# Seven products instead of eight blocks in the second product of a fused attention and MLP kernel, with w_in streamed from DRAM

## The chip, the cores and the metric

The kernel runs on one core of one Trainium2 chip. The metric is device microseconds of one execution. The engines are TensorE (PE; its weight loads are shown as PEld), VectorE (DVE), ScalarE (ACT), GpSimd (POOL, hardly used here) and SyncE (SP, whose queue issues nearly all DMAs).

## The reference

Eight batches, each of 8 heads, 512 tokens and 32 state rows, head width 64. Tokens attend to the state rows and the state rows to the tokens; the results of both stand side by side and go through two products with a mish between them.

```python
# x: [8, 8, 512, 64], state: [8, 8, 32, 64], w_in: [512, 2048], w_out: [2048, 512]
a = softmax(x @ state.T / 8);   xread = a @ state        # tokens read the state
a2 = softmax(state @ x.T / 8);  sread = a2 @ x           # state rows read the tokens
t = concatenate([xread, sread], axis=2)                  # to [8 * 544, 512]
h = t @ w_in
out = (h * tanh(softplus(h))) @ w_out                    # mish, then the second product
```

## The kernel before, in words

The first product is folded: `sw_slice` (PE tiles `swp`) multiplies the state rows of a batch with slices of `w_in`, and `gemm1` (PE tiles `ph`) multiplies the attention weights `ah`/`al` with that. Every operand of a large product is split into a high part in float32r and a low part, and three matmuls (high by high, high by low, low by high) stand for one. The names end in h and l: `swh`/`swl`, `gh`/`gl`, `ah`/`al`.

A batch is worked in eight slots j; a slot holds two of the 16 chunks of 128 columns of d_ff. In a slot PE runs `gemm1` for the slot (12 matmuls of 512 columns), ACT applies mish from the two `ph` banks, DVE casts the high part (`gh<-g`) and subtracts the low part (`gl<-g,gh`) on 128x1024, and PE runs the second product `gemm2` (PE tiles `acc`) of an earlier slot: 4 token tiles x 2 chunks x 3 = 24 matmuls of 512 columns, whose weights (the stationary side) are blocks of `gh`/`gl` and whose moving side is `wo`. The lag is two slots (`LAG`): a slot's `gh`/`gl` have some 8 us between their making and their use. The four `acc` banks hold the four token tiles of a batch over all eight slots.

PE's order is the program's order: the class `InOrder` chains each PE instruction behind the last. For batch 0 the order of DVE and ACT is written out by hand too (the long string of steps); from batch 1 on a scheduler with a timeline of its own orders DVE, ACT and the DMA queue by program order among what it takes to be ready, and `behind(...)` holds single pieces back. At run time each engine works its own list strictly in order.

Beside the products each batch prepares the next one: transposes of x on DVE (`x_turned`, moved by eight DMAs into `x_rows`), scores (PE tile `sc`, in slot 3), two softmaxes (`soft2` after slot 3, `soft1` after slot 4; `soft1` ends with `soft1_a`, which makes `ah`/`al`, double-buffered), 16 small DMAs that turn `e2T` (after slot 5), the state rows' read (`srp`, in slot 3 of the next batch), and the `sw_slice`s: two in slot 3 and two in slot 7. Between batches 6 and 7 the state rows' own product runs as key "s" (`gemm1_s`, PE tiles `ph_s` and `acc_s`). `w_in` stays in SBUF in whole (`w_in_sb`). The tag "raw" has two buffers of 8 KB a partition, for `x_turned`, `x_rows` and the x of the batch after next. The tag "t" has five buffers of 128x512, for the softmaxes' temporaries.

## Time and profile before

| | |
|---|---|
| median of 3 runs | 643.96 us (643.93 to 644.2) |
| span of the profiled execution, first to last instruction | 642.2 us |
| time of the profiled execution beside its span | not recorded apart; the median is 1.7 us above the span |
| PE, PEld, DVE, ACT busy | 635.1, 509.2, 350.8, 256.6 us |
| granted TensorE clock | 1.000 |
| one batch in the steady part (228.1 to 299.7 us) | 71.60 us |
| matmuls of the second product: `acc`, `acc_s` | 1536 and 96, all of 512 columns |

A busy time is the union of an engine's instructions. Matmuls are pipelined, so the time that one takes from the stream is the distance between two starts, not its duration. In a row of the timeline "x4" means four instructions merged, of which the start of the first is given; the start of the next row then ends them.

### The profile page before, as it was taken

The page shows a single profiled execution, that of the slowest core. Times are in us where ns is not written, and L with a number is a line of the kernel's source. Part 1 is how long each engine was busy: PE and PEld are TensorE (multiplying, and loading weights), DVE is VectorE, ACT ScalarE, POOL GpSimd, SP SyncE. Part 2 cuts the span into 40 slices and gives each one's busy share as a digit, 9 for nine tenths or more (in the row PEclk, how much of TensorE's full clock was granted, in tenths as well). Part 3 has the DMA queues.
Part 4 walks back from the last instruction along what each step waited for, and adds up shares of the span by engine and source line. Part 5 has one row for each costly group of instructions (what it writes and reads, how often), then busy time and mean ns, then how long its engine had stood idle before and what let it go on. Part 6 is the DMA issues. An engine that isn't in the chain of part 4 may idle for free.

```text
span 642.2 us, 10938 instructions
## 1 busy us (share of the span) xinstructions
PE 635.1 (99%) x4523; PEld 509.2 (79%) x4523; DVE 350.8 (55%) x564; ACT 256.6 (40%) x419; POOL 0.7 (0%) x6
## 2 busy tenths in 40 slices
PE   8999999999999999999999999999999999999997
PEld 5777787787878888787878788787878788878886
DVE  5999983665339253665349252755359366432222
ACT  4999852542226122532226212622236336221110
POOL 0000000000000000000000000000000000000000
PEclk9999999999999999999999999999999999999999
DMA  8996717210431033211431033211221001000001
GB/s 326 411 322 183 241 41 205 76 33 15 122 106 53 12 74 132 67 33 31 139 94 36 7 75 131 69 31 40 93 76 47 8 0 67 0 17 17 1 0 65
DMA packets 52129, 56.15 MB, mean 87 GB/s; under 512 B 13297, under 2 KB 41713, under 8 KB 52081
## 3 DMA queue, kind: packets, MB, share of 16 engines
q1 hardware_dynamic: 51648, 55.27, 27.4%
q8 instruction: 35, 0.57, 0.4%
q10 hardware_dynamic: 432, 0.20, 0.1%
q14 instruction: 14, 0.11, 0.1%
HBM read 34.54 MB, written 8.91 MB: 68 GB/s over the span
## 4 chain that ended last, share of the span: by engine, by line
PE 98%; DMA 1%; DVE 0%; SPq 0%; ACT 0%; issue 0%
PE acc L70 55%; PE ph L70 27%; PE swp L70 5%; PE ph_s L70 3%; PE acc_s L70 3%; PE sc L70 1%; PE srp L70 1%; DMA x<-in_x_dram 1%; PE scT L70 0%; SPq L131 0%; DVE scs L70 0%; DVE xT L70 0%; DVE al L70 0%; DVE mx L70 0%; ACT o L70 0%; ACT ah L70 0%
## 5 line engine op out<-in xcount | busy, mean ns | idle before, releaser
L70 PE MATMUL acc<-wo,gh 128*128 128x512 f32 x1024 | 317.9, 392 | 0.0
L70 PEld LDWEIGHTS acc<-wo,gh 128*128 128x128 f32 x1024 | 190.7, 188 | 46.1 <-issue 7.0
L70 PE MATMUL acc<-wo,gl 128*128 128x512 f32 x512 | 199.4, 389 | 0.0
L70 ACT ACTIVATE g<-ph 128x512 f32<-128x512 f32 x128 | 73.6, 597 | 216.7 <-DVE gl L70 199.8
L70 DVE CAST gh<-g 128x1024 fp32r<-128x1024 f32 (+1 forms) x61 | 41.3, 678 | 137.8 <-PE acc L70 131.2
L70 PEld LDWEIGHTS acc<-wo,gl 128*128 128x128 f32 x512 | 96.1, 188 | 20.4
L70 DVE TENSOR_TENSOR gl<-g,gh 128x1024 fp32r<-128x1024 f32 (+1 forms) x65 | 78.4, 1207 | 4.6
L70 PE MATMUL ph<-ah,swh 128*128 128x512 f32 (+1 forms) x260 | 79.8, 389 | 0.0
L70 PE MATMUL ph<-al,swh 128*128 128x512 f32 (+1 forms) x260 | 79.4, 387 | 0.2 <-DVE al L70 0.2
L70 PE MATMUL ph<-ah,swl 128*128 128x512 f32 (+1 forms) x260 | 79.5, 387 | 0.0
L70 DVE TENSOR_TENSOR swl<-swp,swh 128x512 fp32r<-128x512 f32 (+1 forms) x72 | 40.9, 624 | 37.3 <-ACT swh L70 37.2
L70 PEld LDWEIGHTS ph<-ah,swh 128*128 128x128 f32 x260 | 48.2, 188 | 11.8 <-issue 1.2
L70 ACT ACT_TABLE_LOAD x35 | 44.9, 1283 | 30.6 <-DVE s L70 15.7
L70 PEld LDWEIGHTS ph<-al,swh 128*128 128x128 f32 x260 | 48.5, 188 | 10.5 <-DVE al L70 0.4
L70 PEld LDWEIGHTS ph<-ah,swl 128*128 128x128 f32 x260 | 48.6, 188 | 10.2
L70 ACT CAST swh<-swp 128x512 fp32r<-128x512 f32 (+1 forms) x72 | 33.9, 549 | 31.8 <-PE swp L70 31.8
L70 PE MATMUL swp<-w_in_sb,bd 64*32 64x256 f32 x1024 | 33.1, 380 | 0.0
L70 DVE COPY o<-acc 128x512 f32<-128x512 f32 x16 | 11.0, 688 | 32.8 <-PE acc L70 20.0
L70 ACT COPY o<-acc 128x512 f32<-128x512 f32 (+1 forms) x17 | 9.5, 563 | 47.7 <-PE acc L70 30.4
L70 PEld LDWEIGHTS swp<-w_in_sb,bd 64*32 64x32 f32 x1024 | 18.1, 106 | 9.5 <-issue 4.3
L70 DVE TENSOR_SCALAR scs<-sc 128x512 f32<-128x512 f32 (+1 forms) x9 | 5.6, 631 | 29.9 <-PE sc L70 29.9
L70 PE MATMUL acc_s<-wo,gh_s 128*128 128x512 f32 x64 | 19.9, 392 | 0.0
(90 smaller groups left out, 430.6 us busy)
## 6 DMA issues: line engine op xcount, KB each, us to landing
x<-in_x_dram SPq DMA_DIRECT2D x32, 256.0 KB, 3.8
...
out_dram<-o SPq DMA_DIRECT2D x31, 256.0 KB, 2.5
x_rows<-x_turned SPq DMA_DIRECT2D x56, 128.0 KB, 2.4
x_in<-in_x_dram SPq DMA_DIRECT2D x24, 256.0 KB, 3.7
e2T<-u SPq DMA_DIRECT2D x128, 32.0 KB, 1.9
x_again<-in_x_dram SPq DMA_DIRECT2D x8, 256.0 KB, 5.5
```

Source lines behind the costliest of these rows:

```text
L70: made = method(*args, **kwargs)
```

## The change

In batches 2 to 7 and in key "s" the second product is made by pairs of token tiles. A unit is one slot of one pair: 2 chunks of d_ff by 2 token tiles, so 2 by 2 blocks of g, against 2 chunks by 2 halves of `wo`. For the slots 0 to 4 (`SEVEN = 5`) the unit is multiplied by the seven products of Strassen's method in Winograd's form: each product has 3 matmuls (the split) of 256 columns, where the unit had 12 of 512. For the slots 5 to 7 a unit keeps its 12 matmuls of 512 columns. `prepare` makes a unit's operands: three sums on DVE, two casts on ACT and two low parts on DVE with seven products; one cast and one low part, both on DVE, without. `gh` and `gl` now hold one unit each and have two buffers.

The four `acc` banks now belong to one pair ("one", "two", "top", "end"), and a sweep goes through all eight slots for one pair, then for the other. So the units of the second pair wait: g is kept as float32 in up to ten buffers (`UNITS`), and mish is four instructions of 256 columns instead of two of 512. At each point where half a slot's second product stood, one unit is now consumed, if one is ready: in batch 2 one a slot from slot 3 on, then two a slot, and ten remain after the last slot of batch 7. After the seven-product slots, four small instructions gather the banks "one" and "two" into `sums`; at the end of a sweep each tile's result is one DVE addition or subtraction instead of a copy.

The sums of the blocks of `wo` (`seven_weights`, for slots 0 to 4) are made in batch 1 from slot 3 on, one slot at a time; they take the place of `w_in_sb`. `w_in` is first written to DRAM (4 DMAs of 1 MB) and then read back in slices of 1 MB, four for each of the batches 2 to 7 and four for "s", mostly through the tag "raw". The `sw_slice`s of slot 3 are spread over slots 3 and 5 in batches 2 to 6. `ah` and `al` lose their second buffer: `soft1_a`, now `soft1_parts`, moves to the end of slot 7, after the last `gemm1` that reads them. `swh`/`swl` have two pairs of buffers. x of the batch after next is loaded after slot 7 instead of slot 5, and `sreads_moved` of batch 6 moves from slot 5 to slot 6.

```diff
+UNITS = 10
+SEVEN = 5
+G = 4 * P
...
-    w_in_sb = const.tile([P, NC, DF], F32, name="w_in_sb")
+    w_in_sb = const.tile([P, NC, DF], F32, tag="w_in", name="w_in_sb")
+    w_in_again = dram.tile([P, NC, DF], F32, name="w_in_again")
...
-                small["a"] = [pool.tile([P, 2, S], F32R, tag=t, name=f"{t}_{b}") for t in ("ah", "al")]
+                small["a"] = [pool.tile([P, 2, S], F32R, tag=t, name=f"{t}_{b}", bufs=1) for t in ("ah", "al")]
...
-            whole(soft1_n(), *(soft1_a(kc) for kc in two))
+            whole(soft1_n())
+        def soft1_parts():
+            whole(*(soft1_a(kc) for kc in two))
...
+    def load_w_in_again(g, tag="raw", bufs=2):
+        w = pool.tile([P, NC, G], F32, tag=tag, name=f"w_in_{g}", bufs=bufs)
+        last["again"] = nc.sync.dma_start(w, w_in_again[:, :, g * G:(g + 1) * G])
+        return w
...
-        hi = pool.tile([P, 2, n * 2 * P], F32R, tag="swh", name=f"swh_{b}_{j}", bufs=3)
-        lo = pool.tile([P, 2, n * 2 * P], F32R, tag="swl", name=f"swl_{b}_{j}", bufs=3)
+        if n == 2 or j % 2 == 0:
+            sw_pairs[b] = [pool.tile([P, 2, 4 * P], F32R, tag=t, name=f"{t}_{b}_{j}") for t in ("swh", "swl")]
+        at = j % 2 * 2 * P
+        hi, lo = (t[:, :, at:at + n * 2 * P] for t in sw_pairs[b])
...
+    def result(key, t, acc, sums=None, op=None):
+        if (key, t) == (B - 1, NT - 1):
+            last_o = pool.tile([P, DM], F32, tag="e2T", name=f"o_{key}_{t}", bufs=1)
+            for i, part in enumerate((slice(0, 256), slice(256, 512))):
+                o = last_o[:, part]
+                dve.tensor_tensor(o, acc[:, part], sums[:, i], op)
+                (nc.scalar if part.start else nc.sync).dma_start(
+                    out[key * T:key * T + S, part].rearrange("(p t) e -> p t e", t=NT)[:, t, :], o)
+            return
+        o = pool.tile([P, DM], F32, tag="o", name=f"o_{key}_{t}", bufs=2)
+        if sums is not None:
+            dve.tensor_tensor(*(a.rearrange("t (h e) -> t h e", h=2) for a in (o, acc)), sums, op)
+        elif t % 2 == 0:
+            dve.tensor_copy(o, acc)
+        else:
+            act.copy(o, acc)
+        store(key, t, o)
...
+    A12, A22, A11, A21 = range(4)
+    S1, S3, S2, S4 = range(3, 7)
+    T3, T4, T2 = range(3)
+    wx = []
+    def seven_weights(j):
+        if not wx:
+            wx.append(const.tile([P, SEVEN, 2, 3, 256], F32R, tag="w_in", name="wx"))
+        w = pool.tile([P, 4, 256], F32, tag="wt", name=f"w_sums_{j}", bufs=1)
+        dve.tensor_add(
+            w.rearrange("p (k e) c -> p k (e c)", k=2), as_f32(wo[j][:, :, 0]), as_f32(wo[j][:, :, 1]))
+        dve.tensor_sub(w[:, 0], w[:, 0], w[:, 1])
+        dve.tensor_sub(w[:, 1], w[:, 3], w[:, 1])
+        dve.scalar_tensor_tensor(w[:, 3], w[:, 3], -1.0, w[:, 0], ALU.mult, ALU.subtract)
+        dve.tensor_add(w[:, 2], w[:, 2], w[:, 3])
+        low, high = (wo[j][:, 0, n, 256:] for n in range(2))
+        act.copy(high, w[:, 0])
+        dve.tensor_sub(low, w[:, 0], as_f32(high))
+        low, high = (wx[0][:, j, n] for n in range(2))
+        act.copy(high, w[:, 1:])
+        dve.tensor_sub(low, w[:, 1:], as_f32(high))
+    def products(j):
+        left, right = slice(0, 256), slice(256, 512)
+        if j < SEVEN:
+            return [
+                (A11, "one", left, wo[j][:, 0, :, left]), (S2, "one", right, wx[0][:, j, :, T2]),
+                (S3, "two", left, wx[0][:, j, :, T3]), (S1, "two", right, wo[j][:, 0, :, right]),
+                (A12, "top", left, wo[j][:, 1, :, left]), (S4, "top", right, wo[j][:, 1, :, right]),
+                (A22, "end", left, wx[0][:, j, :, T4])]
+        return [
+            (a, bank, slice(0, 512), wo[j][:, k])
+            for bank, blocks in (("top", (A11, A12)), ("end", (A21, A22))) for k, a in enumerate(blocks)]
...
+            if key == 1:
+                beside += [sw_slice(key, 4, 2, first_bank, misc), sw_slice(key, 6, 2, misc, first_bank)]
+            else:
+                beside += [sw_slice(key, 4, 2, first_bank, misc, w=wis[key, 2])]
+        if j == 5 and more and key > 1:
+            beside += [sw_slice(key, 6, w=wis[key, 3])]
+        if j == 2 and not more:
+            beside += [sw_slice(key, 4, bank=first_bank, w=wis[key, 2]), sw_slice(key, 6, w=wis[key, 3])]
+        if j == 7 and more:
+            beside += [sw_slice(key + 1, 0, w=wis[key + 1, 0])]
+            beside += [sw_slice(key + 1, 2, bank=first_bank, w=wis[key + 1, 1])]
...
+        if key == 1 and j < 2:
+            for g in range(2 * j, 2 * j + 2):
+                nc.sync.dma_start(w_in_again[:, :, g * G:(g + 1) * G], w_in_sb[:, :, g * G:(g + 1) * G])
+        if key == 1 and 3 <= j < 3 + SEVEN:
+            seven_weights(j - 3)
...
+        if more and key > 1 and j == 2:
+            wis[key, 2] = load_w_in_again(2)
+        if not more and j == 0:
+            wis[key, 2], wis[key, 3] = load_w_in_again(2), load_w_in_again(3)
...
+            if key > 1:
+                wis[key, 3] = load_w_in_again(3)
...
+            wis[key + 1, 0] = load_w_in_again(0)
...
+            wis[key + 1, 1] = load_w_in_again(1)
...
+        if more and j == 7:
+            own["parts"]()
+            if key + 2 < B:
+                load_x_in(key + 2)
...
+    def mish_units(key, j, phs):
+        for p in range(2):
+            u = new_unit(key, p, j)
+            for k, ph in enumerate(phs):
+                last["mish"] = act.activation(
+                    u[:, 1 - k].rearrange("f h t -> f (h t)"), ph[:, p * 2 * P:(p + 1) * 2 * P], AF.Mish)
+    def prepare():
+        if not todo or todo[0] not in made:
+            return
+        unit = todo.pop(0)
+        key, p, j = unit
+        u = made.pop(unit).rearrange("f k h t -> f (k h) t")
+        hi, lo = (pool.tile([P, 7, P], F32R, tag=t, name=f"{t}_{key}_{p}_{j}") for t in ("gh", "gl"))
+        n = 3 if j < SEVEN else 4
+        if j < SEVEN:
+            sums = temp(f"sums_{key}_{p}_{j}").rearrange("f (s t) -> f s t", s=4)
+            dve.tensor_add(sums[:, :2], u[:, 1:3], u[:, 3:].to_broadcast([P, 2, P]))
+            dve.tensor_add(sums[:, 2], sums[:, 0], u[:, 2])
+            dve.tensor_add(sums[:, 3], sums[:, 2], u[:, 0])
+            act.copy(hi[:, :n], u[:, :n])
+            act.copy(hi[:, n:], sums)
+            low_g(u[:, :n], hi[:, :n], lo[:, :n])
+            low_g(sums, hi[:, n:], lo[:, n:])
+        else:
+            dve.tensor_copy(hi[:, :n], u)
+            low_g(u, hi[:, :n], lo[:, :n])
+        parts[unit] = hi, lo
+        ready.append(unit)
...
+    def consume():
+        if not ready:
+            return
+        unit = ready.pop(0)
+        key, p, j = unit
+        hi, lo = parts.pop(unit)
+        if j == 0:
+            spans[key, p] = {n: second_bank(f"acc_{key}_{p}_{n}") for n in ("one", "two", "top", "end")}
+        banks = spans[key, p]
+        for i, (a, bank, to, w) in enumerate(products(j)):
+            for n, (g, h) in enumerate(((hi, 1), (hi, 0), (lo, 1))):
+                fresh = (key, p, bank) not in begun_banks
+                begun_banks.add((key, p, bank))
+                last["PE"] = pe.matmul(
+                    banks[bank][:, to], g[:, a], w[:, h], start=fresh,
+                    stop=(n == 2 and (j == SLOTS - 1 and i % 2 == 1 or j == SEVEN - 1 and i < 4)), skip_group_check=True)
+            e = banks.get("sums")
+            if j == SLOTS - 1 and i == 1:
+                result(key, 2 * p, banks["top"], e[:, ::2], ALU.add)
+            if j == SLOTS - 1 and i == 3:
+                result(key, 2 * p + 1, banks["end"], e[:, 1::2], ALU.subtract)
+        if j == SEVEN - 1:
+            e = spans[key, p]["sums"] = pool.tile([P, 4, 256], F32, tag="wt", name=f"sums_{key}_{p}", bufs=1)
+            one, two = (banks[n].rearrange("t (h e) -> t h e", h=2) for n in ("one", "two"))
+            act.copy(e[:, 0], one[:, 0])
+            dve.tensor_add(e[:, 3], e[:, 0], one[:, 1])
+            dve.tensor_add(e[:, 1:3], two, e[:, 3:].to_broadcast([P, 2, 256]))
+            dve.tensor_add(e[:, 3], e[:, 1], two[:, 1])
+    def two_next():
+        for _ in range(2):
+            if not todo or (ready and todo[0][2] == 0):
+                return
+            prepare()
+    def halves():
+        if pending:
+            return [lambda: second((0, 1), True), lambda: second((2, 3))]
+        return [consume, consume]
+    for key in [*range(2, B - 1), "s", B - 1]:
+        for j in range(4 if key == "s" else SLOTS):
+            one, other = halves()
+            if key == "s":
+                if j == 0:
+                    one()
+                    sread_transposed()
+                    other()
+                for r in range(2):
+                    gemm1_s(j, r, wis["s", j], new_unit("s", 0, 2 * j + r))
+                    if j:
+                        (one, other)[r]()
+                if j < 2:
+                    wis["s", j + 2] = load_w_in_again(j + 2, *(() if j else ("x", 1)))
+            else:
+                mish_units(key, j, gemm1(key, j, aTs[key], sw))
+                one()
+                around(key, j)
+                other()
+                after(key, j)
+            two_next()
+    while ready or todo:
+        while ready:
+            consume()
+        two_next()
```

More of the change, by code (lines that the diff above doesn't have):

```diff
@@ L514, in soft2 @@
                 whole(soft2_e(kc))
-        own.update(soft1=soft1, soft2=soft2, turn=e2_turned)
+        own.update(soft1=soft1, parts=soft1_parts, soft2=soft2, turn=e2_turned)
         return own
@@ L522, in srT_parts @@
     def srT_parts(bs, values):
-        hi, lo = (t[:, :, bs.start * NS:bs.stop * NS] for t in srT)
+        hi, lo = (t[:, :, bs.start * NS:bs.stop * NS] for t in srT[:2])
         act.copy(hi, values)
@@ L540, in sreads_split @@
     def sreads_split():
+        both = pool.tile([P, NC, 2, B * NS], F32R, tag="raw", name="srT", bufs=2)
+        srT.extend(both[:, :, i] for i in range(2))
+        srT.append(both)
         srT_parts(early, srds["moved"].rearrange("p c b n -> p c (b n)"))
@@ new lines, in store @@
+    def store(key, t, o):
+        if key == "s":
+            for b4 in range(4):
+                r0 = (4 * t + b4) * T + S
+                nc.sync.dma_start(out[r0:r0 + NS, :], o[b4 * NS:(b4 + 1) * NS, :])
+        else:
+            to = out[key * T:key * T + S, :]
+            last["store"] = nc.sync.dma_start(to.rearrange("(p t) e -> p t e", t=NT)[:, t], o)
+    def result(key, t, acc, sums=None, op=None):
[15 more added lines that the diff above has]
+        store(key, t, o)
@@ L668, in gemm2 @@
                         start=(fc == 0 and n == 0), stop=(fc == NFC - 1 and n == 2))
[L669 to L689 removed]
+            if fcs[-1] == NFC - 1:
+                result(key, t, accs[key][t])
     raws, rawo, wfull = {}, {}, {}
@@ L890, in state_attention_mish_kernel, with around @@
+    own = at1
+    spans = {}
+    def around(key, j):
+        nonlocal own, prev, sn_next
+        more = key + 1 < B
         if j == 0:
             prev = own
-            if key + 1 < B:
+            if more:
                 own = attention(key + 1, sn_next, x_ins.pop(key + 1))
                 aTs[key + 1] = own["aT"]
-        more = key + 1 < B
         beside = []
@@ L934, in state_attention_mish_kernel @@
                 own["xd"](0)
+        if more and j == 1:
+            with behind("swl"):
+                own["st"](0)
+        if more and key > 1 and j == 2:
+            wis[key, 2] = load_w_in_again(2)
+        if not more and j == 0:
+            wis[key, 2], wis[key, 3] = load_w_in_again(2), load_w_in_again(3)
         if more and j == 3:
@@ new lines, in after @@
+        if key == B - 2 and j == 7:
+            wis["s", 0] = load_w_in_again(0, "x", 1)
+            wis["s", 1] = load_w_in_again(1)
+            with behind("mish", "low"):
+                sreads_split()
+    wis, prev = {}, None
+    for j in range(SLOTS):
+        g = split_g(f"1_{j}", mish(1, j, gemm1(1, j, aTs[1], sw)))
+        pending.append((1, (2 * j, 2 * j + 1), g, NT))
+        slow = j < 2
+        ready = slow or len(pending) > LAG
+        if ready and not slow:
+            second((0, 1), True)
+        around(1, j)
+        if ready:
+            second((2 * j, 2 * j + 1), j == 0) if slow else second((2, 3))
+        after(1, j)
@@ new lines, in state_attention_mish_kernel, with new_unit @@
+    made, parts = {}, {}
+    todo = []
+    for key in [*range(2, B - 1), "s", B - 1]:
+        todo += [(key, p, j) for p in range(1 if key == "s" else 2) for j in range(SLOTS)]
+    def new_unit(key, p, j):
+        made[key, p, j] = pool.tile([P, 2, 2, P], F32, tag="unit", name=f"u_{key}_{p}_{j}", bufs=UNITS)
+        return made[key, p, j]
+    def mish_units(key, j, phs):
[4 more added lines that the diff above has]
+                    u[:, 1 - k].rearrange("f h t -> f (h t)"), ph[:, p * 2 * P:(p + 1) * 2 * P], AF.Mish)
```

141 lines of the change are left out of this document (41 added, 100 removed).

## The prediction

> **What bounds the kernel now.** I read the page first: busy times, the slices, the chain that ended last.
>
> ```profile
> span 642.2 us, 10938 instructions
> ...
> PE 635.1 (99%) x4523; PEld 509.2 (79%) x4523; DVE 350.8 (55%) x564; ACT 256.6 (40%) x419; POOL 0.7 (0%) x6
> ...
> DVE  5999983665339253665349252755359366432222
> ...
> PE 98%; DMA 1%; DVE 0%; SPq 0%; ACT 0%; issue 0%
> PE acc L70 55%; PE ph L70 27%; PE swp L70 5%; PE ph_s L70 3%; PE acc_s L70 3%; PE sc L70 1%; PE srp L70 1%; DMA x<-in_x_dram 1%; PE scT L70 0%; SPq L131 0%; DVE scs L70 0%; DVE xT L70 0%; DVE al L70 0%; DVE mx L70 0%; ACT o L70 0%; ACT ah L70 0%
> ```
>
> PE is 98% of the chain, and `acc` with `acc_s`, the second product, is 58%. A busy PE could still hide waits, so I read the stages next, and PE's timeline for the distance from start to start.
>
> ```profile
> 109.40:156.50 47.10, 47.10 (x405) 37.44 (x404) 27.59 (x49) 19.38 (x31) 0.00 (x0) 1.00 0.20 56
> 228.10:299.70 71.60, 71.60 (x513) 57.73 (x512) 36.84 (x61) 24.03 (x39) 0.00 (x0) 1.00 0.24 69
> 264.90:281.20 16.30, 16.30 (x73) 13.51 (x72) 14.77 (x30) 11.09 (x16) 0.00 (x0) 1.00 0.16 46
> ```
>
> Columns: stretch, its length, then busy us of PE, PEld, DVE, ACT, POOL, clock, DMA share, GB/s. The second row is batch 3, the third its slots 4 and 5, the first is batch 1 from slot 3 on. PE never rests. DVE is half idle over a batch, but 91% busy in slots 4 and 5 (14.77 of 16.30), where the softmax is.
>
> ```profile
> 97.34 1.09 PE L70 MATMUL swp<-w_in_sb,bd 64*32 64x256 f32 x32
> 98.37 0.50 PE L70 MATMUL acc<-wo,gh 128*128 128x512 f32 x1
> ...
> 294.94 1.96 PE L70 MATMUL swp<-w_in_sb,bd 64*32 64x256 f32 x64
> 296.82 0.74 PE L70 MATMUL acc<-wo,gh 128*128 128x512 f32 x2
> ...
> 299.72 0.61 PE L70 MATMUL ph<-ah,swh 128*128 128x512 f32 x2
> ...
> 302.44 0.39 PE L70 MATMUL acc<-wo,gh 128*128 128x512 f32 x1
> ...
> 522.04 0.64 PE L70 MATMUL ph_s<-srT,wl 128*128 128x256 f32 x4
> 522.51 1.09 PE L70 MATMUL ph_s<-srT,wh 128*128 128x512 f32 x4
> ```
>
> The twelve 512-column matmuls of a slot start at 299.72 and end at 302.44: 2.72 us, 0.2267 each. The four of 256 columns, each with weights of its own, take from 522.04 to 522.51: 0.47 us, 0.1175 each, 52% of the long one.
>
> **The change part by part. PE.** A unit of 12 x 0.2267 = 2.72 us becomes 21 x 0.1175 = 2.47 us: 0.25 us less. There are 6 batches x 2 pairs x 5 slots + 5 for key "s" = 65 such units: 16.3 us less. A reading error of 0.01 us over the four short matmuls moves 21 of them by 0.05 us, so the bounds are 13 and 19.5 us; I keep 16. The units of slots 5 to 7 cost what they cost. Splitting the slices of slot 3 over slots 3 and 5: a group of 32 takes 98.37 - 97.34 = 1.03 us, one of 64 takes 296.82 - 294.94 = 1.88, so two groups cost 0.18 more, and twice the step to the next product (0.1 each, an estimate from the 0.50 and 0.74 of the rows behind `swp`, against 0.39 and 0.61 in the rows within a run): 0.3 us x 5 batches = 1.5 us. PE's work: 16 - 1.5 = 14.5 us less.
>
> Can the weight loads keep pace? A unit loads 21 blocks instead of 12.
>
> ```profile
> L70 PEld LDWEIGHTS ph_s<-srT,wl x64: 187/188/192, 521.8 to 554.2; 128*128 128x128 f32 x64
> ```
>
> A load lasts 188 ns and still one matmul starts every 117.5 ns, so loads overlap with each other and with matmuls. The Trainium skill ("TensorE: Matmul & The Clock Gate", Part 3, The mechanism) says that a weight load overlaps running matmuls only if it goes to another row group, and (LDWEIGHTS) that 128 columns load in 128/1.2 = 107 ns. By that, nine more full-height loads a unit would cost 9 x 107 ns = 0.96 us, 62 us in all, and the change would lose. The trace does not bear it out: 512-column matmuls come every 226.7 ns, which leaves some 13 ns beyond the page's own 213 ns of streaming (512 columns at 2.4 GHz). The same page's Part 2 has the load pulled ahead into a background buffer, and with that the trace agrees. What stays open is a run of 21 instead of 4; it is a rival below.
>
> **DVE and ACT.**
>
> ```profile
> L70 DVE TENSOR_TENSOR gl<-g,gh 128x1024 fp32r<-128x1024 f32 x8 | 9.8, 1225 | 0.6
> L70 DVE CAST gh<-g 128x1024 fp32r<-128x1024 f32 x8 | 5.5, 686 | 16.8 <-PE acc L70 16.8
> L70 DVE TENSOR_TENSOR swl<-swp,swh 128x512 fp32r<-128x512 f32 x8 | 5.0, 684 | 6.5 <-ACT swh L70 6.5
> L70 DVE COPY o<-acc 128x512 f32<-128x512 f32 x2 | 1.4, 693 | 4.6 <-DMA out_dram<-o 2.4 <-PE acc L70 2.2
> L70 DVE STREAM_TRANSPOSE at<-e 128x512 f32<-128x512 f32 x2 | 1.3, 686 | 0.0
> L70 DVE TENSOR_TENSOR al<-at,ah 128x512 fp32r<-128x512 f32 x2 | 1.3, 688 | 0.2 <-ACT ah L70 0.2
> ...
> L70 ACT ACTIVATE g<-ph 128x512 f32<-128x512 f32 x16 | 9.2, 597 | 28.6 <-DVE gl L70 27.8 <-PE ph L70 0.4
> L70 ACT ACT_TABLE_LOAD x4 | 5.1, 1283 | 5.1 <-DVE s L70 2.6 <-DVE nm L70 1.7 <-DVE gl L70 0.7
> ...
> L70 ACT COPY g_s<-ph_s x16: 366/372/388, 522.8 to 554.7; 128x256 f32<-128x256 f32 x16
> L70 DVE TENSOR_TENSOR g_s<-g_s,ph_s x16: 411/416/425, 523.2 to 555.1; 128x256 f32<-128x256 f32 x16
> ```
>
> A seven-product unit on DVE: a sum of 256 elements 0.42, two of 128 at most 0.42 each (I take 0.3), low parts of 384 (between 0.42 and 0.69: 0.55) and 512 (0.69): 2.3 us. A plain unit: cast 0.4 (half of 0.686 to all of it) and low part 0.69: 1.1 us. A sweep's end: three small sums 1.5, two results 1.4. A steady batch: 36.84 - 9.8 - 5.5 - 1.4 + 10 x 2.3 + 6 x 1.1 + 2 x 2.9 = 55.5 us of 71.6 - 10 x 0.25 + 0.3 = 69.4 us, 80%. ACT: mish is 32 of 256 at about 0.4 instead of 16 of 0.597, +3.3; casts of 384 and 512 for ten units, at 0.5 and 0.6, +11; without the two copies of `o`: about 37 of 69. No engine passes PE on average, so what counts is where a unit is late.
>
> The cover shrinks: before, a slot's parts were made some 8 us ahead; now a unit's parts wait for one of two buffers. The next unit but one has 2.5 to 2.7 us of another unit and 2.72 us of `gemm1`, 5.2 us in all, for two casts on ACT and the low parts on DVE behind them, about 2.1 us. Alone that fits. Places where DVE is taken:
>
> Slots 4 and 5 of batches 3 to 6: 14.77 less two slots' parts (3.8) and `soft1_a` (1.3 + 1.3), plus four seven-product units 9.2, two results 1.4 and two `swl` 1.4: 20.4 us for PE's 2 x 2.72 + 2.72 + 2.72 + 2 x 2.47 + 1.1 = 16.9. 3.5 us too many, of which the 2.72 us of `gemm1` at the start of slot 6, and whatever runs early in slot 3, take most. Wait a batch: 0 to 3.5, taken 0.6, nearer to nothing because sums need no free buffer and slot 6 has only one seven-product unit: 2.4 us.
>
> Batch 2 consumes one unit a slot from slot 3, made in the slot before, so slots last 5.2 us, and mish (2 x 0.4), sums, casts and low parts (together some 4.2) must fit into that while `soft1` holds DVE: 0 to 5, taken 2.
>
> Batch 1 gets `seven_weights`: five times one sum of 1024 (1.2), four of 256 (1.7), one low part of 256 (0.4) and one of 768 (0.95) = 4.2 us: 21 us, on DVE's 27.59 of 47.10: 48.6, full. What is late is the last in program order: `ah`/`al` of batch 2, or the first units: 0 to 5, taken 1.5.
>
> The five borders into batches 2 to 6: `ah`/`al` have one buffer, so two casts and two subtractions come after slot 7's `gemm1` and before the next. Cover on PE: two units and two slices, 2.47 + 1.88 + 2.72 = 7.1 us; work ahead of them on DVE: `swl` 2.5, `sums` 1.5, one unit 1.1, `al` 1.3 = 6.4. 0 to 1 each, taken 0.2: 1. The start of "s", the border after batch 0 and the last ten units: 0 to 3, taken 0.6. Waits together: 7.5 us, between 0 and 32.
>
> **DMA.** 4 MB are written and 28 MB read more.
>
> ```profile
> x_rows<-x_turned SPq DMA_DIRECT2D x56, 128.0 KB, 2.4
> x_in<-in_x_dram SPq DMA_DIRECT2D x24, 256.0 KB, 3.7
> ...
> 230.37 5.21 SPq L300 DMA_DIRECT2D x_rows<-x_turned  x8
> 246.88 1.97 SPq L131 DMA_DIRECT2D x_in<-in_x_dram  x4
> ...
> 259.35 0.69 DVE L70 TENSOR_SCALAR scs<-sc 128x512 f32<-128x512 f32 x1 [4.69 <-PE sc L70]
> ```
>
> Four x_in of 256 KB are issued in 1.97 us and land 3.7 after issue: 1 MB in some 5.7 us. Four slices a batch: 23 us of 69. The tightest is the one for slots 4 and 5: its buffer is free when `x_rows` has landed (230.37 + 5.21 + 2.4 = 238.0), so it is there at about 244, and PE wants it behind `sc`, at about 259. 15 us of cover, 9 in batch 2 with its short slots; SP issues one for 0.65 us (5.21 / 8). Cost: nothing. If the cover went, 5.7 us in each of five batches, 28 us.
>
> **Sum.** Against the profiled execution: span 642.2 - 14.5 + 7.5 = 635.2; what lies around it, 1.7 us to the median of 643.96, stays: 637 us.
>
> **The rivals.** Within 0.2% (1.3 us) is no change; that is what a measurement of this kernel can tell.
>
> A, DVE sets the pace in bursts: the next unit's low parts stand behind the softmax, and PE waits in every batch. For it: 20.4 us in 16.9, and 48.6 in 47.1. Against it: 80% on average, and most casts on ACT, which has room. With all upper bounds it is 629.5 + 32 = 661; at half, 645.5. It decides from 14.5 us of waits on, 2.4 us in each of six batches.
>
> B, the waits are all hidden, as in the trace of before, where 71.60 of 71.60 us are PE: 629.5 us, 628 to 633.
>
> C, the slices of `w_in` come late, because SP stands at a load whose buffer is not free and everything behind it waits: 28 us, 665. Against it: the 15 us.
>
> D, the change doesn't do what it says: in long runs of 256 columns the loads set the pace. At the 188 ns of a load a unit takes 3.95 us, 80 us more in all; from 2.72 / 21 = 129.5 ns on nothing is saved. Against it: 117.5.
>
> **How the numbers follow.** Forecast (some waits, 633 to 642.6) 0.48, B 0.22, A 0.22 (of which 0.06 within 0.2%), C 0.05, D 0.03. Faster 0.48 + 0.22 = 0.70, same 0.06, slower 0.24. The range 629.5 to 650 leaves out the lower part of B (0.05), the upper half of A (0.06), C and D: 0.19. The likeliest one's own range is 633 to 642.6.
>
> **What would show it.** PE: units of 21 short matmuls in 2.47 us, batches 3 to 5 at 69.4 us plus waits. DVE near 80% in a steady batch. Waits of PE's `acc` for DVE low parts, in slots 4 to 6 and in batch 2, and of `ph` for `al` at the borders. No wait of `swp` for a DMA. I am wrong if the short matmuls come slower than every 120 ns, if a steady batch takes over 71.6 us, or if PE waits for a load.

## Result: 2.9% slower, with the time lost in one batch and at four other places

The changed kernel takes 662.67 us (661.25 to 663.16) against 643.94 (643.81 to 644.2) of the kernel before, measured together: ratio 1.029 [1.0276, 1.0305]. Forecast were 637.0, and 629.5 to 650. The profiled execution took 661.25 us with a span of 659.5, against 642.2 before. Lines of the page of after:

```profile
span 659.5 us, 12906 instructions
...
PE 633.3 (96%) x5108; PEld 529.1 (80%) x5108; DVE 461.9 (70%) x951; ACT 333.3 (51%) x654; POOL 0.7 (0%) x6
...
PE   8999999999996899999999999999999899999997
...
PEclk9999999999996999999999999999999999999999
...
PE 77%; DVE 10%; DMA 6%; ACT 4%; issue 2%; SPq 1%; DVEq 0%; ACTq 0%
```

PE is 77% of the chain instead of 98%: it now waits. The slices show one deep dent, the 13th, at 198 to 214 us, and the granted clock dips there too. That is batch 2. The rows by stage, of before (batch 2, and from the last `gemm1` to the end):

```profile
156.51:228.11 71.60, 71.60 (x513) 57.71 (x512) 36.84 (x61) 23.93 (x39) 0.00 (x0) 1.00 0.24 69
...
619.20:642.20 23.00, 19.24 (x85) 15.58 (x84) 5.22 (x6) 2.43 (x5) 0.00 (x0) 1.00 0.12 46
```

and of after (batch 2, a part of it, batch 4, and from the last `gemm1` to the end):

```profile
159.99:231.74 71.75, 61.40 (x497) 50.28 (x497) 45.54 (x104) 32.80 (x70) 0.00 (x0) 0.93 0.40 121
194.45:210.00 15.55, 9.34 (x38) 7.94 (x37) 14.79 (x38) 10.66 (x17) 0.00 (x0) 0.67 0.58 196
300.88:372.73 71.85, 70.64 (x602) 60.35 (x602) 50.26 (x115) 35.26 (x75) 0.00 (x0) 1.00 0.42 128
621.25:659.50 38.25, 34.39 (x212) 30.70 (x210) 18.40 (x35) 7.26 (x16) 0.00 (x0) 1.00 0.07 28
```

The end is 15.2 us longer: ten units stand there instead of four half slots, six units of 2.5 us more. They come from batch 2 (five fewer consumed than before) and batch 3 (one fewer). So batch 2 should last about 71.6 - 5 x 2.72, some 58 us. It lasts 71.75. The work was moved out of it, and the time stayed.

The table sums up where each span went, by the starts of `gemm1` of the batches (b0 to b7), of the first `ph_s` (s) and of the last `gemm1` (tail). Medians and ratios are those of all runs, the stages those of the profiled one; e14's profiled execution, at 646.79 us, is the fastest of its four.

| kernel | median us, ratio to before | b0 | b1 | b2 | b3 | b4 | b5 | b6 to s | s | b7 | tail |
|---|---|---|---|---|---|---|---|---|---|---|---|
| before | 643.94 | 89.1 | 67.4 | 71.6 | 71.6 | 71.6 | 71.6 | 78.2 | 38.8 | 59.3 | 23.0 |
| after | 662.67, 1.029 | 90.9 | 69.1 | 71.8 | 69.1 | 71.9 | 71.9 | 80.9 | 38.4 | 57.5 | 38.2 |
| e1_slack | 661.31, 1.0267 [1.0251, 1.0284] | 91.1 | 69.1 | 67.8 | 71.9 | 71.9 | 71.9 | 80.8 | 38.4 | 57.5 | 38.2 |
| e2_prep_first | 665.5, 1.033 [1.0305, 1.0355] | 90.4 | 69.1 | 73.3 | 69.0 | 71.7 | 71.7 | 83.6 | 38.5 | 57.5 | 38.2 |
| e3_seven0 | 663.97, 1.0307 [1.0291, 1.0322] | 91.1 | 67.4 | 67.0 | 71.1 | 72.0 | 72.0 | 84.1 | 38.9 | 59.3 | 39.4 |
| e4_double | 744.86, 1.156 [1.1539, 1.1582] | 159.1 | 83.9 | 72.0 | 69.3 | 71.9 | 71.9 | 80.8 | 38.6 | 57.5 | 38.4 |
| e5_filler | 673.26, 1.0446 [1.0422, 1.0471] | 91.4 | 69.1 | 82.1 | 70.8 | 71.9 | 71.9 | 80.8 | 38.4 | 57.5 | 38.2 |
| e6_resident0 | 657.57, 1.0199 [1.0171, 1.0227] | 88.7 | 67.4 | 68.9 | 69.4 | 72.0 | 72.0 | 79.7 | 38.9 | 59.3 | 39.3 |
| e7_three | 660.49, 1.0249 [1.0224, 1.0275] | 88.8 | 72.4 | 72.4 | 69.2 | 72.1 | 71.9 | 78.7 | 38.4 | 57.5 | 38.2 |
| e8_pool_sums | 662.28, 1.0281 [1.0252, 1.0309] | 90.5 | 69.1 | 70.5 | 69.6 | 70.6 | 70.6 | 84.5 | 37.9 | 57.5 | 38.2 |
| e9_early_softmax | 655.59, 1.0179 [1.0161, 1.0197] | 91.4 | 69.1 | 63.5 | 69.1 | 72.1 | 71.9 | 82.3 | 38.6 | 57.5 | 38.2 |
| e10_around_first | 656.32, 1.0188 [1.0169, 1.0208] | 92.1 | 69.1 | 65.5 | 69.1 | 72.1 | 71.9 | 80.9 | 38.4 | 57.5 | 38.2 |
| e11_all | 647.13, 1.0045 [1.003, 1.006] | 89.1 | 68.0 | 62.1 | 68.0 | 70.6 | 70.6 | 82.2 | 37.9 | 57.5 | 38.2 |
| e12_all_dve | 645.76, 1.0025 [1.0016, 1.0035] | 88.3 | 68.0 | 61.0 | 69.2 | 71.9 | 71.9 | 78.8 | 38.4 | 57.5 | 38.2 |
| e13_mixed | 644.04, 1.000 [0.9991, 1.0009] | 88.5 | 68.0 | 60.1 | 68.0 | 70.6 | 70.6 | 82.6 | 38.4 | 57.5 | 38.2 |
| e14_repaired_seven0 | 649.78, 1.0097 [1.008, 1.0114] | 88.4 | 67.4 | 58.6 | 69.4 | 72.0 | 72.0 | 79.7 | 38.9 | 59.3 | 39.4 |
| e15_moved_only | 644.29, 1.0007 [0.9996, 1.0017] | 88.6 | 68.0 | 60.1 | 68.0 | 70.6 | 70.6 | 81.9 | 38.6 | 57.5 | 38.2 |
| e16_moved_dve6 | 640.69, 0.9953 [0.9941, 0.9965] | 88.8 | 68.0 | 60.2 | 68.0 | 70.6 | 70.6 | 78.7 | 38.4 | 57.5 | 38.2 |

**Batch 2, slot 4.** PE's timeline of after:

```profile
196.56 0.40 PE L73 MATMUL acc_one<-wo,gh 128*128 128x256 f32 x2
196.80 0.28 PE L73 MATMUL acc_one<-wo,gl 128*128 128x256 f32 x1
201.81 0.79 PE L73 MATMUL acc_one<-wx,gh 128*128 128x256 f32 x2 [4.73 <-ACT gh L73]
204.08 0.58 PE L73 MATMUL acc_one<-wx,gl 128*128 128x256 f32 x1 [1.48 <-DVE gl L73]
...
207.66 1.05 PE L73 MATMUL ph<-ah,swh 128*128 128x512 f32 x2
...
211.31 0.40 PE L73 MATMUL acc_one<-wo,gh 128*128 128x256 f32 x2
```

and what ACT does meanwhile:

```profile
195.37 0.66 ACT L73 ACTIVATE u<-ph 128x256 f32<-128x256 f32 x2 [1.52 <-PE ph L73]
196.05 1.28 ACT L73 ACT_TABLE_LOAD   x1
197.34 0.72 ACT L73 ACTIVATE e<-scs,nm 128x512 f32<-128x512 f32 x1
...
198.88 1.28 ACT L73 ACT_TABLE_LOAD   x1
200.18 0.66 ACT L73 ACTIVATE u<-ph 128x256 f32<-128x256 f32 x2
200.72 0.52 ACT L73 CAST gh<-u 128x384 fp32r<-128x384 f32 x1
201.12 0.63 ACT L73 CAST gh<-sums 128x512 fp32r<-128x512 f32 x1
201.77 1.28 ACT L73 ACT_TABLE_LOAD   x1
```

The unit that PE wants at 197 needs two casts. On ACT's list they stand behind the softmax's exponentials and two table loads of 1.28 us, and are done at 201.8: PE waits 4.73 us (4.89 counted from start to start, as in most comparisons below). The low part on DVE then costs 1.48 more. During the wait the clock is halved, from 199.4 us on for 10.2 us (0.67 on average in the row 194.45 to 210.00): the `gemm1` at 207.66 takes until 211.31, 3.65 us instead of 2.72. The rest of batch 2: twice 0.8 us where `gemm1` stands directly behind an `sw_slice` with no second unit between them, 2.75 us at its border to batch 3 (`ph` for `swl`), and some 2.8 us by the clock (0.93 in that `gemm1`, 1.9 in the unit before it): 13.8 us together by the starts of PE's groups, against the 13.6 moved out.

**The other places.** The timelines of DVE at the borders from batch 1 to 2 and behind batch 4, of ACT ahead of "s", and of SP in batch 0 and ahead of "s":

```profile
156.91 1.28 DVE L73 TENSOR_TENSOR swl<-swp,swh 128x512 fp32r<-128x512 f32 x2
158.11 1.22 DVE L73 TENSOR_TENSOR w_sums<-wo 128x1024 f32<-128x1024 f32 x1
159.24 1.29 DVE L73 TENSOR_TENSOR swl<-swp,swh 128x512 fp32r<-128x512 f32 x2
...
370.59 1.28 DVE L73 TENSOR_TENSOR swl<-swp,swh 128x512 fp32r<-128x512 f32 x2
371.79 0.28 DVE L73 TENSOR_TENSOR sums<-sums,u 128x128 f32<-128x128 f32 x1
371.99 1.28 DVE L73 TENSOR_TENSOR swl<-swp,swh 128x512 fp32r<-128x512 f32 x2
```
```profile
517.88 0.62 ACT L73 CAST wh<-w_in 128x512 fp32r<-128x512 f32 x1 [3.57 <-DMA w_in<-w_in_again]
518.42 1.07 ACT L73 CAST swh<-swp 128x512 fp32r<-128x512 f32 x2
```
```profile
41.22 0.54 SPq L967 DMA_DIRECT2D w_in_again<-w_in_sb  x1
41.85 6.58 SPq L177 DMA_DIRECT2D wir<-in_moe_w_in_dram  x4
...
512.19 1.74 SPq L564 DMA_DIRECT2D w_in<-w_in_again  x2
```

At 158.11 a sum for the new weights is put between the two pairs of `swl` that batch 2's first `gemm1` needs, and `gemm1` waits 1.7 us. In the steady batches sums of later units stand ahead of `swl` (0.88 us at each border), and in slot 5 a `gl` is late behind the softmax (0.65). Ahead of "s" the cast of a slice of `w_in` that was issued at 512.19 and has not landed holds ACT for 3.57 us, and `swh`, which PE wants, stands behind it: that stage is 2.65 us longer. In batch 0 the writes of `w_in` to DRAM were placed among its first loads: 1.8 us.

### The profile page after: what moved, and what is told of

It reads as the page before. It is cut to its first block, busy times and chain, and to the rows that moved or that the text cites. A ratio compares the mean times of both kernels' runs of the same rounds, so it can differ in the third digit from the quotient of the medians.

```text
span 659.5 us, 12906 instructions
## 1 busy us (share of the span) xinstructions
PE 633.3 (96%) x5108; PEld 529.1 (80%) x5108; DVE 461.9 (70%) x951; ACT 333.3 (51%) x654; POOL 0.7 (0%) x6
## 4 chain that ended last, share of the span: by engine, by line
PE 77%; DVE 10%; DMA 6%; ACT 4%; issue 2%; SPq 1%; DVEq 0%; ACTq 0%
PE ph L73 23%; PE acc_top L73 12%; PE acc L73 9%; PE acc_end L73 9%; PE acc_two L73 6%; PE acc_one L73 6%; DMA wir<-in_moe_w_in_dram 3%; PE swp L73 3%; PE ph_s L73 3%; DVE gl L73 2%; DVE sums L73 2%; DVE swl L73 1%; DMA wor<-in_moe_w_out_dram 1%; PE srp L73 1%; PE sc L73 1%
## 5 line engine op out<-in xcount | busy, mean ns | idle before, releaser
L73 ACT ACTIVATE u<-ph 128x256 f32<-128x256 f32 x192 | 63.7, 384 | 107.8 <-PE ph L73 104.0
L73 DVE TENSOR_TENSOR gl<-u,gh 128x384 fp32r<-128x384 f32 (+1 forms) x96 | 58.1, 606 | 73.7 <-ACT gh L73 72.1
L73 PE MATMUL acc_top<-wo,gh 128*128 128x256 f32 (+1 forms) x384 | 91.8, 327 | 1.0 <-DVE gh L73 1.0
L73 PE MATMUL ph<-ah,swh 128*128 128x512 f32 (+1 forms) x260 | 82.1, 396 | 8.6 <-DVE swl L73 6.4
L73 PE MATMUL acc<-wo,gh 128*128 128x512 f32 x256 | 80.0, 393 | 0.0
L73 PEld LDWEIGHTS acc_top<-wo,gh 128*128 128x128 f32 x384 | 64.0, 192 | 9.4 <-DVE srds L73 1.6
L73 PE MATMUL acc_top<-wo,gl 128*128 128x256 f32 (+1 forms) x192 | 62.4, 325 | 0.5 <-DVE gl L73 0.5
L73 PEld LDWEIGHTS acc<-wo,gh 128*128 128x128 f32 x256 | 47.4, 188 | 12.7 <-issue 2.9
L73 ACT ACT_TABLE_LOAD x35 | 44.9, 1283 | 13.8 <-DVE nm L73 7.0
L73 PE MATMUL acc<-wo,gl 128*128 128x512 f32 x128 | 49.9, 390 | 0.0
L73 PE MATMUL acc_end<-wo,gh 128*128 128x512 f32 x144 | 44.4, 389 | 0.0
L73 DVE TENSOR_TENSOR gl<-sums,gh 128x512 fp32r<-128x512 f32 x60 | 41.5, 691 | 0.0
## 6 DMA issues: line engine op xcount, KB each, us to landing
wir<-in_moe_w_in_dram SPq DMA_DIRECT2D x16, 512.0 KB, 10.2
```

What stands on the lines that cost most here:

```text
L73: made = method(*args, **kwargs)
```

## Experiments

The theory: the seven products do what they should, and the time is lost because the units are deferred, so that PE has too little other work in batch 2 while a unit's casts wait in ACT's list. Rivals: the pair-wise order has the wrong place for making units; the sums on DVE are the bound; the streaming of `w_in` costs it.

**One unit fewer a slot**, in batch 2 from slot 2 on.

```diff
+            if key == 2 and j > 1:
+                other = lambda: None
```


> Edit: in batch 2 no second consumption from slot 2 on, so that each unit is prepared two slots ahead of its use instead of one; nothing is left out. T1 (units late behind the softmax on DVE and ACT, worst in batch 2, where a unit is made, prepared and used within one slot; the wait then lowers the granted clock): the wait of the unit in slot 4 of batch 2 (some 7 us, and 2 us of slow clock behind it) goes, 653 +- 2 us. T2 (the w_in slices and the DMAs behind them are late): 662 +- 2. T3 (short matmuls slower in long runs): 662.

Measured: 661.31 us. Slot 4 of batch 2 falls from 14.24 to 6.79 us, but slots 5 to 7 last 10.33, 10.1 and 9.7: the waits are now 3.69 us (`ph` for ACT's `swh`), 1.88 within the `gemm1` behind it and 2.28 at the border (both for `swl`), and 1.16 (for `u`), and the clock is halved for 6.8 us from 209.1 on. Batches 2 and 3 together gain 1.2 us. Consuming less only moves the wait to the next users of the lists of ACT and DVE.

**Units made before the slot's other preparations.**

```diff
                 other()
+                two_next()
                 after(key, j)
-            two_next()
+            if key == "s":
+                two_next()
```


> Edit: the preparation of the next two units stands ahead of the next batch's softmax and transposes in program order, instead of behind; nothing else. T1 with the list order as the cause (DVE has the sums of unit 3 of batch 2 listed behind the maxima of the softmax): the same 9 us go, and part of the 0.8 us waits in slot 5 and the 0.9 us at the border of each steady batch: 650 +- 3 us. T1 with too much work as the cause (DVE full, whatever the order): the softmax is late in its place, 660 +- 3. T2, T3: 662 +- 2.

Measured: 665.5 us, slower than after. The wait of 4.89 us becomes 1.18 + 2.58, and slots 5 and 6 lose more than slot 4 gained (13.18 and 10.88 instead of 8.08 and 5.84). The units' place in the lists alone is not the cause: the waits change places.

**Without the seven products** (pairs, deferral and streaming kept; the results are then plain copies of the banks).

```diff
-SEVEN = 5
+SEVEN = 0
```


> Edit: SEVEN = 0, so every unit is 12 matmuls of 512 columns with one cast and one low part, no sums of weights; the sweeps by pairs, the units, the streamed w_in, the single ah and al and ten units at the end stay. Seven products save 65 x 0.2 = 13 us of PE and cost their preparation. T1: without sums and casts of sums the waits mostly go: 643.9 + 1.5 (slices split) + 2 (early writes of w_in) + 3 (start of the state rows' product, its w_in late) + 3 for batch 2 = 653 +- 3, so that the seven products as such lose 9. T2: the waits stay, 662.7 + 13 = 675. T3: 662.7 + 65 x 0.05 less = 660 or so with no waits in batch 2.

Measured: 663.97 us. That is none of the three times expected. With no seven-product unit in it, the kernel is as slow as after: its span is 19.9 us above before, 2 of them for the split slices, so some 18 us are lost to the order by pairs and to the streaming alone. The seven products bring 1.3 us, though with them PE's work is some 14 us less: most of what they save is lost again.

**`w_in` copied once more in DRAM ahead of each read**, to double the streaming.

```diff
+        copies.append(dram.tile([P, NC, G], F32, name=f"copy_{len(copies)}", tag=f"copy_{len(copies)}"))
+        nc.sync.dma_start(copies[-1], w_in_again[:, :, g * G:(g + 1) * G])
```


> Edit: each of the 28 reads of a 1 MB slice of w_in is followed by a copy of the same 1 MB from DRAM to a DRAM tile that nobody reads; the traffic of the streaming is doubled. T1: the time stays within 3 us of 662.7, most of it at the start of the state rows' product. T2: each load and the moves behind it are some 3 to 5 us later: 28 x 0.3 and more, 670 to 690.

Measured: 744.86 us, but it doesn't test what it should: the copies were all issued in the first 170 us, and PE waits 33.7 us up to 107.7, 20.6 up to 146.1 and 12.1 up to 188.9, all ahead of batch 2. From batch 2 on the stages are those of after within 0.3 us, without any added traffic there. Nothing follows for the streaming.

**More work for PE in batch 2**: `gemm1` of slots 3 to 7 repeats its matmuls, 5 x 12 x 0.2267 = 13.6 us.

```diff
+            if b == 2 and j > 2 and i == 0:
+                for n in range(6):
+                    pe.matmul(ph, *phs[k][1][n], start=(n == 0), stop=(n == 5), skip_group_check=True)
```


> Edit: in slots 3 to 7 of batch 2, where the second half of the second product is missing, each gemm1 is run once more ahead of itself into the same banks and overwritten: 5 x 12 matmuls of 512 columns, 13.6 us of PE, without use. T4 (batch 2 has given five units to the end of the kernel, but its slots do not get shorter, since each waits for ACT and DVE; so the deferred 13.6 us are paid twice): the added work is free, 663 +- 3 us, and the granted clock stays up. T3 or any theory by which PE sets the pace in batch 2: 676. If longer slots also let the late parts catch up, less than 662.

Measured: 673.26 us; batch 2 is 10.3 us longer, so the added work was not free. Had its waits been idle time spread over the slots, the filler would have been free. Only the wait in slot 4 took some of it (4.89 to 2.05 us); 0.8, 0.8 and 2.75 stay as they were, since what they wait for starts only after the matmuls ahead of them.

**Without the seven products, and with `w_in` resident.** Beside `SEVEN = 0`:

```diff
-        w = pool.tile([P, NC, G], F32, tag=tag, name=f"w_in_{g}", bufs=bufs)
-        last["again"] = nc.sync.dma_start(w, w_in_again[:, :, g * G:(g + 1) * G])
-        return w
+        return None
```


> Edit: SEVEN = 0 as in the kernel with plain units (663.97 us), and w_in stays in SBUF: no writes to DRAM, no slices read back, all else kept. T5 (streaming is what the change lost): batch 0 back by 1.8 us, the start of the state rows' product by 5, some of batch 2: 650 or less. T4: batch 2 keeps its 9 us, only batch 0 and the start of the state rows' product come back: 657 +- 2.

Measured: 657.57 us, 6.4 less than e3_seven0. Batch 0 gives 2.4 and the stage ahead of "s" 4.4, the two places named above; batches 2 and 3 together give 0.3 the other way. So, with plain units, streaming costs at its two ends and not in the stream.

**Three holds**: the writes of `w_in` in batch 1 slot 1, the fifth set of sums in batch 2, the casts `wh` behind `swh`.

```diff
-            act.copy(hi, w)
+            with behind("swh"):
+                act.copy(hi, w)
...
+        if key == 2 and j == 0:
+            with behind("swl"):
+                seven_weights(4)
```


> Three edits that touch three different stages, with five of seven products kept: the writes of w_in to DRAM held back until batch 1's slot 1; the sums of wo[4] moved behind the low parts of the slices at the border into batch 2; the casts of w_in in the state rows' product listed behind those of the slices on ACT. Expected by stages: batch 0 -1.8 us, batch 1 -1.7, batch 6 to the state rows -2; sum 657 +- 1.5. If the writes are not what slows batch 0, its 90.9 us stay; if the late slice itself and not the place of its cast is what holds the state rows' product, that stage keeps its 80.8 us.

Measured: 660.49 us. Batch 0 -2.1, the wait at the border into batch 2 0.57 instead of 1.71, the stage ahead of "s" -2.1: each hold did its part. But batch 1 is 3.2 us longer: four writes of 1 MB at once delayed the small DMAs of `e2T` there, `srp` waited 2.50 us for them, and the clock was halved for 3.4 us.

**The units' sums on GpSimd.**

```diff
-            dve.tensor_add(sums[:, :2], u[:, 1:3], u[:, 3:].to_broadcast([P, 2, P]))
+            pool_e.tensor_add(sums[:, :2], u[:, 1:3], u[:, 3:].to_broadcast([P, 2, P]))
```


> Edit: the three sums of a seven-product unit are made on GpSimd instead of DVE, nothing else. If DVE's list (sums standing between the steps of the softmax) makes the units late: the wait in slot 4 of batch 2 shrinks by 3 to 7 us and the 0.65 us in slot 5 and 0.9 us at the border of each steady batch mostly go: 653 +- 4. If GpSimd is slow (over 2 us for the three) the units are later: 670. If the waits come from ACT's order (table loads, exponentials ahead of the casts): 662.

Measured: 662.28 us. The wait in slot 4 of batch 2 is the same 4.89 us for ACT's `gh`. The trace of after alone could not tell ACT from DVE there, since DVE's last sum of that unit (first row) is done only just before ACT's cast of 201.12. Here GpSimd has the sums of the unit ready at 189.26, and ACT's cast still comes at 200.73 (the other two rows). So ACT's list alone is enough for the wait.

```profile
200.78 0.25 DVE L73 TENSOR_TENSOR sums<-sums,u 128x128 f32<-128x128 f32 x1
```
```profile
188.03 1.23 POOL L73 TENSOR_TENSOR sums<-sums,u 128x128 f32<-128x128 f32 x2
...
200.73 0.63 ACT L73 CAST gh<-sums 128x512 fp32r<-128x512 f32 x1
```

The waits of the steady batches go, 1.3 us in each. Batch 6 loses 3.6. Groups of this run by form, on POOL and DVE, and the DVE groups of after:

```profile
L73 POOL TENSOR_TENSOR sums<-sums,u 128x128 f32<-128x128 f32 x120 | 72.0, 609 | 6.3
L73 POOL TENSOR_TENSOR sums<-u 128x256 f32<-128x256 f32 x60 | 49.3, 828 | 475.3 <-ACT u L73 213.3 <-DVE gl L73 117.9 <-DVE u L73 57.9
L73 DVE TENSOR_TENSOR gl<-sums,gh 128x512 fp32r<-128x512 f32 x60 | 44.4, 739 | 1.2 <-ACT gh L73 1.0
```
```profile
L73 DVE TENSOR_TENSOR gl<-sums,gh 128x512 fp32r<-128x512 f32 x60 | 41.5, 691 | 0.0
L73 DVE TENSOR_TENSOR sums<-sums,u 128x128 f32<-128x128 f32 x120 | 31.8, 287 | 0.6
L73 DVE TENSOR_TENSOR sums<-u 128x256 f32<-128x256 f32 x60 | 24.4, 421 | 8.0 <-ACT u L73 7.8
```

**The softmax of batch 2 two slots earlier**, while the plain units of batch 1 are still there as cover.

```diff
-        if j == 3 and more:
+        if j == (1 if key == 2 else 3) and more:
...
-        if more and j == 3:
+        if more and j == (1 if key == 2 else 3):
...
-        if more and j == (2 if key == 2 else 4):
```
(and the same for the pieces ahead of and behind it)

> Edit: in batch 2 alone, scores and softmaxes for batch 3 stand two slots earlier (scores in slot 1 instead of 3), where the leftover of batch 1 still gives each slot 8.2 us; nothing else. T6 (the burst of the softmax, on ACT with its exponentials and four table loads as much as on DVE, meets slots of 5.2 us whose unit is made, prepared and used at once; it is the burst's place and not an order within it): slot 4 of batch 2 falls from 14.2 to some 5.5 us, slots 1 to 3 get at most 2 us longer, the half clock goes; batch 2 from 71.8 to 63, the kernel 654 +- 2. If batch 2 is short of something else in every slot (DVE in all, or the buffers): the wait moves along, as with the earlier edits, 660 +- 2.

Measured: 655.59 us, 7.1 less than after, and batch 2 is 8.3 us shorter. Its whole row, and the waits that are left in it:

```profile
160.56:224.03 63.47, 59.08 (x498) 47.79 (x498) 44.88 (x104) 32.68 (x70) 0.00 (x0) 1.00 0.45 135
```
```profile
PE ph L73 <- DVE swl L73: 4.2, 2, 2.7
PE ph L73 <- ACT swh L73: 1.5, 2, 0.7
PE acc_one L73 <- DVE gl L73: 0.2, 1, 0.2
```

The same work on the same engines: the clock is 1.00 instead of 0.93, slot 4 lasts 5.64 us instead of 14.24, and the wait for `gh` is gone. The cause is the burst of the softmax at a place with one unit a slot. This run moves the burst's steps on DVE along with those on ACT; that ACT's list alone makes the wait is what e8_pool_sums showed. Left is what the slices and the border cost.

**In batch 2 the unit behind the slices instead of ahead of them.**

```diff
+                if key == 2 and j > 2:
+                    around(key, j)
+                    one()
```


> Edit: in slots 3 to 7 of batch 2 the slices and scores come ahead of the slot's one unit on PE instead of behind it. T7 (with the second unit missing, gemm1 follows a slice at once and waits for its casts and low parts: 0.8 us twice and 2.75 us at the border to batch 3): these go, but slot 4's wait stays: 658.5 +- 1.5. If ACT or DVE is behind anyway at these places, the waits only change their name: 662.

Measured: 656.32 us, 2 less than expected. The two waits of 0.8 us go and the border falls from 2.75 to 1.10; slot 4 still waits 3.21 + 1.22 us (4.73 + 1.48 in after), and the clock is halved for 6.8 us instead of 10.2.

**All repairs together**, with the sums on GpSimd (e11), on DVE (e12) and mixed (e13: GpSimd in batches 3 to 5, the second pair of batch 2 and the first of batch 6). The four writes are now issued behind the `e2T` copies.

> All at once: early softmax in batch 2, slices first in batch 2, the writes of w_in behind the last move of e2T in batch 1, the sums of wo[4] behind the border's low parts, the state rows' casts behind the slices', sums of the units on GpSimd. By T6 and T7 and the stages measured before: batch 0 -2.1, border into batch 2 -1.1, batch 2 -8 to -12, steady batches -1.27 each of three, state rows -2.1: 662.7 - 17 to -21 = 642 to 646, level with the kernel before. If the waits are one backlog that moves on, above 652.

> As the one with all edits, but with the sums of the units on DVE: the difference is what GpSimd's sums are worth. Expected 1.27 x 3 + some 1 us above it, 646 to 651; if GpSimd's sums hurt at the state rows (as they did there alone, +3.6), level or below.

> As the kernel with all edits and DVE sums (645.76 us), but the units of batches 3 to 5, the second pair of batch 2 and the first pair of batch 6 have their sums made on GpSimd. If the steady waits (0.65 us before the first unit of slot 5, 0.88 us at the border) come from DVE's list alone: steady batches 70.6 instead of 71.9, batch 3 68.0 instead of 69.2, batch 6 keeps its 78.8: 645.8 - 1.2 - 2.6 - 0.7 = 641.2 +- 1, faster than the kernel before. If GpSimd's slower sums only move the waits to the state rows, as they did alone: 645 +- 1.

Measured: 647.13, 645.76 and 644.04 us; e11 and e13 miss their main expectations. Batch 2 is down to 60 to 62 us, near the 58 worked out above. With GpSimd the steady batches are 70.6 instead of 71.9, but the stage ahead of "s" is 82 instead of 79.

**The repaired kernel without the seven products.**

> As the kernel with all edits and DVE sums, with SEVEN = 0: plain units, no sums of weights. Before the repairs the seven products were worth 664.0 - 662.7 = 1.3 us. If what ate them were their own preparation, the repairs of the order in batch 2 give them back only in part: 645.8 + 13 - (steady waits 1.5 x 4) - 1 = 652 +- 2, so they are worth some 6 us. If the repairs help plain units as much: 646 to 648.

Measured: 649.78 us, so the seven products are now worth 4.0 us by the medians (2.0 by the two spans, 645.0 and 643.0). Its steady batch has no wait of PE and lasts 72.00, against 71.60 of before: the split slices cost 0.4. With the seven products on DVE it is 71.86: of the 2.1 us saved on PE, all but some 0.1 are lost to waits, most of them for DVE.

**`sreads_moved` of batch 6 back in slot 5** (e15), and the sums of that batch on DVE as well (e16). In e13 a copy on ACT waits 5.6 us for the DMAs that read `sr_turned`, whose buffer it takes.

```diff
-        if key == B - 2 and j == 6:
+        if key == B - 2 and j == 5:
...
-            adder = pool_e if key in (3, 4, 5) or (key, p) in ((2, 1), (6, 0)) else dve
+            adder = pool_e if key in (3, 4, 5) or (key, p) == (2, 1) else dve
```


> One edit to e13_mixed: sreads_moved of batch 6 goes from slot 6 back to slot 5, where the kernel before has it. Theory (the shared buffer): in e13_mixed the stage from batch 6 to the start of s lasts 82.56 us against 78.79 of e12_all_dve, because ACT waits 5.61 us in a sums<-acc_one for a DMA that reads sr_turned, and sums and sr_turned share one buffer. With the move one slot earlier that DMA is done when sums is written: the stage at 78.5 to 79.5, the kernel at 640 to 641.5 us, ratio 0.995, and the rest of the ledger as in e13_mixed. Rival (the stage is long because six of its sums run on GpSimd, late): the stage stays at 82 to 83 and the kernel at 644. Third: sreads_moved in slot 5 stands ahead of the batch's softmax on DVE and the wait only moves there: 642 to 644.

> As e15_moved_only, and the sums of the first pair of batch 6 are on DVE as well, so that only batches 3 to 5 and the second pair of batch 2 have theirs on GpSimd. Theory (the shared buffer): it differs from e15_moved_only by less than 1 us, 640 to 641.5. Rival (GpSimd's sums in batch 6): 640 to 641.5 here, and e15_moved_only at 644. If both stay at 644, neither is the cause.

Measured: 644.29 and 640.69 us. My theory fell: the earlier slot alone changes nothing, since the DMAs are issued at the same time. SP's rows of e15 and then of e16:

```profile
477.62 0.58 SPq L564 DMA_DIRECT2D w_in<-w_in_again  x1
478.24 1.26 SPq L401 DMA_DIRECT2D e2T<-u  x2
484.17 11.08 SPq L544 DMA_DIRECT2D sr_moved<-sr_turned  x16
```
```profile
472.64 5.69 SPq L401 DMA_DIRECT2D e2T<-u  x8
478.43 0.58 SPq L564 DMA_DIRECT2D w_in<-w_in_again  x1
479.65 10.85 SPq L544 DMA_DIRECT2D sr_moved<-sr_turned  x16
```

In e15 a slice of 1 MB got ahead of the last two small `e2T` copies, and SP then stood 4.3 us at `sr_moved` for them. With the sums on DVE the copies are issued first, and `sr_moved` starts 4.5 us sooner. The granted clock adds to it: in e15 it is halved from 505.1 to 508.5 us, in e16 it is not. That the order on SP is what the sums change is read from these rows. That the slot matters little is seen in e12, which has all sums on DVE and keeps slot 6: its stage ahead of "s" is 78.8 us, against 78.7 of e16. e16 is the fastest of the kernels, 0.5% faster than before.

## Why the prediction was wrong, step by step

- **A unit in 2.47 us**: right in kind. In batch 4 of after a unit starts at 319.67 and the next at 322.18:

```profile
319.67 0.40 PE L73 MATMUL acc_one<-wo,gh 128*128 128x256 f32 x2
...
322.18 0.40 PE L73 MATMUL acc_one<-wo,gh 128*128 128x256 f32 x2
```

  21 matmuls in 2.51 us are 0.1195 each, not 0.1175: four matmuls were a short ruler. By pairs (5.03 instead of 5.44 us) and single units (2.60 instead of 2.82) ten units save 2.1 us, 65 of them some 14 us instead of 16, within the bounds. Rival D is out: 21 loads in a row keep pace. By the overlap rule weighed in the prediction (the Trainium skill, "TensorE: Matmul & The Clock Gate", Part 3, The mechanism) they could not; over the long run, too, the measurement decides against it.
- **The split slices, 0.3 a batch**: 0.4.
- **DVE at 55.5 us a steady batch**: 50.3. ACT at 37: 35.3. The averages were good, and told nothing of the loss.
- **Waits together, 7.5 us**: this is the term that failed. The span grew by 17.3 while PE's work fell by some 14 - 2 = 12 us, so 29 us went to waits and the half clock, near the upper bound of 32, but not where the bounds put them. **Batch 2, "0 to 5, taken 2"**: 13.8. The prediction held mish, sums, casts and low parts of one unit against a slot of 5.2 us, with the softmax on DVE alone, and said of ACT that it "has room". ACT's own share of the softmax was put at nothing there, though its four table loads stand in a row that the prediction shows; and a slot has four mish of 0.38 us, not two. What the runs showed in its place is ACT working its list in order: two table loads and the exponentials stand ahead of the casts, and the only cover was the one unit a slot that the deferral leaves. And the sum had no term for the clock, which cost some 2.8 of the 13.8. The Trainium skill ("TensorE: Matmul & The Clock Gate", Part 1, What's actually happening) puts the drop to half speed at one idle window of about 3.4 us. The 10.2 us are three such windows, but the trace asks for less idle time: the half clock began at 199.4, 2.3 us after the last matmul's end at 197.08.
- **The ten last units**: beyond some waits among them (within "0 to 3, taken 0.6") they had no cost in the sum, as work that is only moved. That holds only if the batch they leave becomes shorter. Here five of the six moved units were paid twice, at the end and as waits in batch 2.
- **Batch 1, 1.5 taken**: 1.7, of which 1.1 by the last sum between the `swl` (0.57 stay in e7_three without it). **Slots 4 and 5 of the steady batches, 0.6**: 0.65. **Borders, 0.2 each**: 2.75 into batch 3 and 0.88 into 4 to 6. The sums of later units, needing no free buffer, were held to be harmless; they stand ahead of `swl`, and `swl` is what `ph` waits for there, not `al`. With this a steady batch takes 71.85 us, over the 71.6 that the prediction named as a sign of being wrong.
- **DMA, "Cost: nothing"**: right for the stream in the batches (no `swp` of batches 2 to 5 waits for a DMA), wrong at its ends: 1.8 us in batch 0, 2.65 ahead of "s". The writes had not been costed at all, and the four slices of "s" have no cover of 15 us.
- **Rivals**: A named waits for DVE in every batch and 661 us as its end. The time is near that, the mechanism only in part: the steady batches do wait for DVE, but 1.5 us each are below its 2.4, and nearly half of the loss lies in one batch, most of it behind a wait for ACT. That the measured time falls on 661 is chance. C's 28 us for late slices did not come.
